# Alternating output banks, two held-back output products and ScalarE's order in block 0, in a fused attention and Strassen MLP kernel

## The chip, the cores and the metric

The kernel runs on one core of one Trainium2 chip. The metric is the device time of one execution in microseconds (us). All times below are in us unless marked otherwise. In times of the trace, zero is the start of the first instruction.

## The reference

The first half is a linear attention without softmax, with a norm per head. Its output is the input of a two-layer MLP with a leaky ReLU.

```python
kv  = einsum('bhsd,bhse->bhde', k, v)          # B=8, H=8, S=576, D=64
o   = einsum('bhsd,bhde->bhse', q, kv)
rms = sqrt(mean(o * o, axis=-1) + 1e-6)
x   = (o / rms * g_norm)                       # -> (B*S, H*D) = (4608, 512)
h   = x @ w_in                                 # w_in (512, 2048)
g   = maximum(0.01 * h, h)
out = g @ w_out                                # w_out (2048, 512)
```

q, k, v and g_norm arrive as float32. The two weight matrices arrive as float64 and the kernel rounds them to float32 itself.

## The kernel before

**Blocks.** The 4608 rows are cut into nine blocks of 512 rows. A *block* goes through the MLP while the attention for the next one is computed in between. All TensorE matmuls are issued through one helper (L118), which pins them: TensorE runs them in exactly the order of the program text. On the other engines a scheduler orders the instructions, apart from those wrapped in `pin(...)`, which keep program order among themselves on their engine.

**Block 0** (`first_block`, L880) is computed directly, in 16 *units* of 128 hidden columns. For unit n TensorE makes `h_ps` (the unit's hidden values, four matmuls of 128x512), ScalarE applies the leaky ReLU (`Prelu`, L898) and writes `g`, and TensorE then adds the unit's part of the output into four accumulators `o_acc`. The program order on TensorE is h_ps of unit n+1, then o_acc of unit n, and so on. So the Prelu of unit n has the time of one o_acc and one h_ps to finish.

**What runs beside block 0.** `between(n, half)` (L922) is called twice per unit. It rounds the weights: each of 32 *roundings* (`round_f64`, L229) takes two ScalarE instructions (`add`, L242, and `cut`, L244) on a raw tile that SP's queue has loaded (L220), and four VectorE instructions (L246, L250, L252, L255). The ScalarE and VectorE instructions of the roundings are pinned. The buffers between the two engines hold four roundings, and the raw tiles hold seven. The loop asks for six roundings after unit 1, three after each of units 2 to 5, then two. `between` also advances the attention of rows 512 to 1151 (`outputs`, L341, and `divide`, L357): TensorE makes `o_ps` (and earlier `kv_ps` from k and v), ScalarE squares it (L349) and scales it (L355), VectorE adds, transposes and reduces the squares (L353, L363, L364), ScalarE takes the root (L367), VectorE the reciprocal (L369), ScalarE spreads it (L373), VectorE transposes and multiplies (L379, L381). L349 and L355 are not pinned. The loads of q, k and v for pairs of heads are on SP's queue too, in program order with the weight loads.

**Blocks 1 to 8** use Strassen's scheme with seven products in place of eight. The 2048 hidden columns are cut into four *chunks*. For each chunk there are seven hidden products (`product_h` for block 1, `product_h_two`, a second level of the scheme, for the others) and seven output products (`product_o`, L836). Both come in the order 1, 2, 6, 5, 7, 3, 4. In the main loop a hidden product and an output product of an earlier chunk alternate, one of each per *slot* (28 slots per block). Output products wait in `o_queue` and are started by `go_o` (L958), with a lag of two slots.

**The banks of the output.** `strassen` (L735) gets two names of PSUM banks. Products 1, 6, 7 and 4 write into the first, products 2, 5 and 3 into the second. Products 1, 2 and 5 start a bank afresh, the others go on in it. After each product VectorE (or, for a chunk's first use in a block, ScalarE, L851) reads the bank and adds it to the output tiles (L582). Before the change the first bank is o_a and the second o_c for every chunk except the very last, which uses hd and hc, two banks of the hidden products. So from chunk to chunk products 4 and 1 use the same bank one after the other.

**The end of a chunk.** When the seven hidden products are done, VectorE combines them, ScalarE applies the leaky ReLU, and GpSimd makes four sums of the result, `gs` (`sums_of`, L760). Products 6, 5, 7 and 3 of the output need these sums; products 1 and 2 don't. In the last block, nothing but output products is left for TensorE after the last hidden product. Loads of the sums of w_out for a later product (`pairs<-w`, L618, on SP's queue) are issued when products 5 and 4 have been read.

Of the kernel before, what the change touches and what calls it, by code (L numbers as in the profile page):

```python
# [12 lines left out]
AF = mybir.ActivationFunctionType  # L13
# [10 lines left out]
def kernel(  # L24
# [36 lines left out]
    nc = tc.nc  # L61
    B, H, S, D = q.shape
# [8 lines left out]
    NB = B * S // NT  # L71
    N2 = NT // 2
    U = 2
    NC = DF // 2 // (U * P)
    SLOPE = 0.01
# [14 lines left out]
    pin = tc.keep_in_program_order  # L90
# [194 lines left out]
    eps_sb = consts.tile([P, 1], F32, name="eps_sb")  # L285
# [40 lines left out]
    def t2k(n, name):  # L326
        home = {"tag": name, "bufs": 1} if name[:3] == "sum" else {"tag": "t2k", "bufs": 3}
        return work.tile([P, n], F32, name=name, **home)

    def x_of(lo, hi):  # L330
        return block(lo // NT)[:, :, lo % NT:lo % NT + hi - lo]
# [25 lines left out]
    def divide(lo, hi, sums):  # L357

        x, n = x_of(lo, hi), hi - lo
        rms = work.tile([P, 2, n // E], F32, tag="rms", name="rms", bufs=2)  # L360
        for l in range(2):
            t = t2k(n, "turned")
            in_turn(nc.vector.transpose(t, sums[l]))  # L363
            in_turn(nc.vector.tensor_reduce(rms[:, l, :], t.rearrange("p (a i) -> p a i", i=E),  # L364
                                            axis=AX.X, op=ALU.add))
            if l:
                nc.scalar.activation(rms, rms, func=AF.Sqrt, scale=1.0 / D, bias=eps_sb)  # L367
            yield
        in_turn(nc.vector.reciprocal(rms, rms))  # L369
        spread = []  # L370
        for l in range(2):
            t = t2k(n, "spread")
            nc.scalar.copy(t.rearrange("p (a i) -> p a i", i=E),  # L373
                           rms[:, l, :].unsqueeze(2).to_broadcast([P, n // E, E]))
            spread.append(t)
        yield
        for l in range(2):
            inv = t2k(n, "inv")
            in_turn(nc.vector.transpose(inv, spread[l]))  # L379
            to = x[:, 2 * l:2 * l + 2, :]  # L380
            in_turn(nc.vector.tensor_mul(to, to, inv.unsqueeze(1).to_broadcast([P, 2, n])))  # L381
            yield
# [453 lines left out]
    def product_o(n, g_sides, os, finish):  # L836
        c = n % NC
        w_sides, _ = sides_w2(n)
        sums = sides_w2(n + 1)[1] if n + 1 < NC * (NB - 1) else lambda i: None
        if c == 0:  # L840
            for key in ("11", "12", "21", "22"):
                os[key] = opool.tile([P, 2, N2], F32, tag="o", name=f"o{key}", bufs=6)

        into = {1: ("11", True), 5: ("22", True), 2: ("11", False), 6: ("12", True),
                3: ("12", False), 7: ("22", False), 4: ("21", True)}

        def done(i, bank):
            key, fresh = into[i]
            to = os[key].rearrange("p u (v n) -> p (u v) n", v=2)
            if c == 0 and fresh:  # L850
                nc.scalar.copy(to, bank)  # L851
            else:
                add(nc.vector, to, bank, to)
            if c == NC - 1 and i in (2, 7, 3, 4):
                finish(key, os[key])

            if i == 5:
                sums(0)
            elif i == 4:
                sums(1)  # L860


        yield from strassen(("oa", "oc") if n + 1 < NC * (NB - 1) else ("hd", "hc"), lambda i, part, r: g_sides[i][:, 2 * r + part, :],
                            lambda i, part, r: w_sides[i][:, r, :], done)

    def go(steps, n=None):
# [13 lines left out]
    def first_block(between):  # L880

        accs = [ps_m.tile([P, DM], F32, tag=t, name="o_acc") for t in ("oa", "oc", "hb", "hd")]
        x, last = xTs.pop(0), None
        for n in range(2 * NC * U + 1):
            now = last
            if n < 2 * NC * U:
                c, h, u = n // (2 * U), n // U % 2, n % U
                h_ps = ps_m.tile([P, NT], F32, tag=("ha", "hc")[n % 2], name="h_ps")

                parts = 2 if n == 0 else 1  # L890
                for part in range(parts):
                    cols = slice(part * NT // parts, (part + 1) * NT // parts)
                    for e in range(NE):
                        matmul(h_ps[:, cols], lhsT=w1_sb[h][c][:, u, e, :],
                               rhs=x[:, e, cols], start=(e == 0 and part == 0),
                               stop=(e == NE - 1), skip_group_check=True)
                gT = view(g_all[n // 4 % 2], n % 4 * NT, NT)
                nc.scalar.activation(gT, h_ps, func=AF.Prelu, alpha=SLOPE)  # L898
                last = (gT, w2_sb[h][c][:, u, :], n)
            if now is None:  # L900
                continue
            between(n, 0)
            for t in range(4):
                matmul(accs[t], lhsT=now[0][:, t * P:(t + 1) * P], rhs=now[1],
                       start=(now[2] == 0), stop=(n == 2 * NC * U))
            between(n, 1)
        for t in range(4):
            o = opool.tile([P, DM], F32, tag="o", name="o", bufs=6)
            if t % 2:
                nc.scalar.copy(o, accs[t])  # L910
            else:
                nc.vector.tensor_copy(o, accs[t])
            nc.scalar.dma_start(out[t * P:(t + 1) * P, :], o)
# [39 lines left out]
    LATE_SLOTS = (3, 4)  # L953

    LAG = 2
    o_queue, waited = collections.deque(), 0

    def go_o():  # L958
# [5 lines left out]
    for i in range(1, NB):  # L964
        one = i == 1
        steady = not one
        late, a_steps = a_steps, attention(i + 1, fine=not one) if i + 1 < B else iter(())
        os = {}
        for c in range(NC):
            g_sides = {}  # L970
            h_steps = product_h(c, h_sides, x_sides, g_sides) if one else \
                product_h_two(i, c, quarters, g_sides)
            for t in range(7):
                slot = 7 * c + t
                go(h_steps, 1)
                if not one:

                    if t == 6:
                        go(h_steps, 1)
                    if slot in LATE_SLOTS:  # L980
                        go(late, 1)
                    for _ in range(FINE_SLOTS.get(slot, 0)):
                        go(a_steps, 1)
                    if i + 1 < NB:
                        if slot == 20:
                            x_sides, new_quarters, sums, inner = sides_x(i + 1)
                        if slot in (20, 21, 22):
                            go(sums, 2 if slot == 20 else 1)
                        if slot == 24:
                            inner(0)  # L990
                        elif slot == 25:
                            inner(1)
                    load_some()
                if waited == LAG:
                    go_o()
                elif o_queue:
                    waited += 1
                if one:

                    if t == 1:  # L1000
                        combine(c, 2)
                    if t == 3 and c < NC - 1:
                        h_sides, more_h = sides_w1(c + 1)
                        combine(c + 1, 0)
                    if t == 5 and c < NC - 1:
                        more_h()
                        combine(c + 1, 1)
                    if slot == 4:
                        go(late, 1)
                    if slot in A_SLOTS:  # L1010
                        go(a_steps, 1)
                    load_some()
                    if slot == 24:
                        go(a_steps)
                        x_sides, new_quarters, sums, inner = sides_x(i + 1)
                        go(sums)
                    elif slot == 25:
                        inner(0)
                    elif slot == 26:
                        inner(1)  # L1020
            if i == NB - 1 and c == NC - 1:
                go(h_steps, 1)
                go_o()
            go(h_steps)
            if c == NC - 1 and i + 1 < NB:
                inner(2)
                quarters = new_quarters
            if one:
                read((2, 4, RING, RING)[c])
            o_queue.append(product_o((i - 1) * NC + c, g_sides, os, store(i)))  # L1030
    while go_o():
        pass
# [30 lines left out]
```

## Time and profile before

| | |
|---|---|
| median of three executions | 942.53 (942.1 to 942.6) |
| the profiled execution: its own time | 942.25 |
| the profiled execution: its span | 940.5 |
| mean granted TensorE clock | 0.998 |
| TensorE busy | 920.1 |
| VectorE busy | 616.0 |
| ScalarE busy | 327.5 |
| GpSimd busy | 317.7 |

The profile comes from one execution, taken by the hardware profiler. A row of the timeline has the start, the time, the engine (PE is TensorE, PEld its weight loads, DVE VectorE, ACT ScalarE, POOL GpSimd, SP the queue of the DMAs), the source line, the operation and what it writes and reads by the program's names, with the idle time before it and who ended that in brackets. A row of the waits has the engine with the tile and line that waited, who it waited for, the total in us, the number of times, and the longest. A row of the windows has the stretch and its length, the busy time and instructions of TensorE, its weight loads, VectorE, ScalarE and GpSimd, then the granted share of the TensorE clock, the share of the DMA engines and the GB/s. The granted clock tells how fast TensorE was allowed to run, 1.00 being full speed.

### The profile page before, as it was taken

What the parts mean: (1) busy time and instruction counts of PE and PEld (TensorE: products, weight loads), DVE (VectorE), ACT (ScalarE), POOL (GpSimd) and SP (SyncE); (2) the same over time, 40 slices, a digit from 0 to 9 for tenths busy, and PEclk for the clock granted to TensorE, in tenths of its full rate; (3) what the DMA queues carried; (4) which work ended last, traced back from release to release, by engine and by line L of the source; (5) the groups of instructions that cost most, each with busy time, mean ns of one, the idle gap of its engine ahead of it and who ended that gap; (6) DMA issues with size and microseconds to landing.
All of it is one profiled execution on the core that took longest, in us unless ns stands there. A gap on an engine that the chain in (4) does not pass through costs nothing.

```text
span 940.5 us, 17989 instructions
## 1 busy us (share of the span) xinstructions
PE 920.1 (98%) x7076; PEld 779.1 (83%) x7076; DVE 616.0 (65%) x992; ACT 327.5 (35%) x659; POOL 317.7 (34%) x318
## 2 busy tenths in 40 slices
PE   7999999999999999999999999999999999999997
PEld 5544447788998899889998999989988999899996
DVE  3866994576457876587657865687558745654554
ACT  3544633242134332533343323342344232223320
POOL 2000364977522532236221611172225322532222
PEclk9999999999999999999999999999999999999999
DMA  8989916885598679856895589658755675567632
GB/s 271 246 211 220 267 61 188 275 296 163 181 312 260 182 211 304 257 164 200 286 287 173 171 280 297 193 169 262 236 154 176 196 219 188 174 199 220 187 108 67
DMA packets 90067, 200.05 MB, mean 213 GB/s; under 512 B 9856, under 2 KB 42112, under 8 KB 89984
## 3 DMA queue, kind: packets, MB, share of 16 engines
q1 hardware_dynamic: 79392, 186.85, 66.3%
q10 hardware_dynamic: 10144, 10.88, 3.4%
q8 instruction: 56, 0.92, 0.4%
q0 software_dynamic: 448, 1.18, 0.3%
q14 instruction: 27, 0.22, 0.1%
HBM read 172.39 MB, written 26.48 MB: 211 GB/s over the span
## 4 chain that ended last, share of the span: by engine, by line
PE 86%; DVE 8%; DMA 3%; issue 1%; POOL 1%; ACT 1%; SPq 0%; DVEq 0%; ACTq 0%; POOLq 0%
PE o_a L118 21%; PE o_c L118 17%; PE h_ha L118 10%; PE h_hc L118 8%; PE h_hb L118 7%; PE h_hd L118 6%; PE o_acc L118 4%; PE h_ps L118 4%; PE kv_ps L118 2%; PE h_c L118 2%; PE h_d L118 2%; PE o_ps L118 1%; PE h_a L118 1%; DMA pairs<-in_v_dram 1%; DVE o L582 1%
## 5 line engine op out<-in xcount | busy, mean ns | idle before, releaser
L582 POOL TENSOR_TENSOR gs<-g 128x512 f32<-128x512 f32 x64 | 81.3, 1289 | 446.7 <-ACT g L753 446.7
L582 DVE TENSOR_TENSOR o<-o_c,o 128x512 f32<-128x512 f32 x85 | 58.5, 688 | 108.2 <-PE o_c L118 108.1
L753 ACT ACTIVATE g<-g 128x512 f32<-128x512 f32 x124 | 78.2, 631 | 122.9 <-DVE g L582 122.9
L118 PE MATMUL o_a<-pairs,gs 128*128 128x256 f32 x496 | 117.3, 379 | 0.0
L582 DVE TENSOR_TENSOR o<-o_a,o 128x512 f32<-128x512 f32 x100 | 68.7, 687 | 71.2 <-PE o_a L118 71.1
L817 ACT COPY w_all<-h_ha 128x512 f32<-128x512 f32 x84 | 48.7, 580 | 189.8 <-PE h_ha L118 181.0
L118 PEld LDWEIGHTS o_a<-pairs,gs 128*128 128x128 f32 x496 | 90.0, 190 | 9.9
L118 PE MATMUL o_a<-w,g 128*128 128x256 f32 x248 | 59.9, 384 | 4.7 <-DVE o L582 4.1
L118 PEld LDWEIGHTS h_ha<-stage,w_all 128*128 128x128 f32 x448 | 58.8, 192 | 2.9
L118 PE MATMUL o_c<-w,g 128*128 128x256 f32 x248 | 59.7, 383 | 0.0
L118 PE MATMUL o_c<-pairs,gs 128*128 128x256 f32 x248 | 59.2, 381 | 0.0
L118 PE MATMUL o_a<-pairs,g 128*128 128x256 f32 x248 | 59.2, 381 | 0.0
L118 PE MATMUL h_ha<-stage,w_all 128*128 128x128 f32 x448 | 59.0, 275 | 0.0
L118 PE MATMUL o_acc<-w,g 128*128 128x512 f32 x128 | 58.3, 598 | 0.7 <-ACT g L898 0.7
L118 PE MATMUL o_c<-w,gs 128*128 128x256 f32 x248 | 58.7, 379 | 0.0
L118 PE MATMUL h_ps<-xT,w_all 128*128 128x512 f32 (+1 forms) x136 | 57.9, 570 | 0.2 <-DVE w_all L255 0.2
L582 DVE TENSOR_TENSOR g<-g,pairs 128x512 f32<-128x512 f32 x84 | 55.6, 689 | 1.9
L118 PEld LDWEIGHTS o_a<-w,g 128*128 128x128 f32 x248 | 44.9, 190 | 13.9 <-DVE o L582 7.8
L582 POOL TENSOR_TENSOR pairs<-w_all 128x512 f32<-128x512 f32 x8 | 11.1, 1383 | 125.7 <-ACT cut L244 106.9
L118 PEld LDWEIGHTS o_c<-w,g 128*128 128x128 f32 x248 | 44.9, 190 | 8.4 <-issue 3.1
L118 PEld LDWEIGHTS o_a<-pairs,g 128*128 128x128 f32 x248 | 45.0, 190 | 6.5 <-DVE w_all L582 0.9
L118 PEld LDWEIGHTS o_c<-pairs,gs 128*128 128x128 f32 x248 | 44.9, 190 | 6.5 <-issue 1.4
(202 smaller groups left out, 1980.6 us busy)
## 6 DMA issues: line engine op xcount, KB each, us to landing
w_all<-w SPq DMA_DIRECT2D x196, 448.0 KB, 4.1
pairs<-w SPq DMA_DIRECT2D x56, 512.0 KB, 4.4
out_dram<-o ACTq DMA_DIRECT2D x36, 256.0 KB, 4.6
v_in<-in_v_dram SPq DMA_DIRECT2D x29, 288.0 KB, 5.3
k_in<-in_k_dram SPq DMA_DIRECT2D x28, 288.0 KB, 5.8
q_in<-in_q_dram SPq DMA_DIRECT2D x56, 144.0 KB, 6.1
q_in<-in_q_dram SPq DMA_DIRECT2D x56, 140.0 KB, 6.0
w<-stage SPq DMA_DIRECT2D x12, 512.0 KB, 4.5
```

The source lines that it names most:

```text
L118: pin(nc.tensor.matmul(*args, **kw))
L582: ins = eng.tensor_tensor(out_, a, b_, op=ALU.subtract if minus else ALU.add)
L753: nc.scalar.activation(t, t if src is None else src, func=AF.Prelu, alpha=SLOPE)
L817: nc.scalar.copy(q[:, at], banks[tag])
```

## The change

It has three parts. The output's two banks swap their roles from chunk to chunk, and the last chunk uses the same two banks as all others. In the last block, slots 22 and 25 start no output product, so the queue is two products longer when the hidden products end. And two kinds of ScalarE instruction are pinned: the Prelu of block 0 (L898) and the root of the norm (L367), which runs in all blocks.

```diff
@@ divide
             if l:
-                nc.scalar.activation(rms, rms, func=AF.Sqrt, scale=1.0 / D, bias=eps_sb)
+                pin(nc.scalar.activation(rms, rms, func=AF.Sqrt, scale=1.0 / D, bias=eps_sb))
@@ product_o
-        yield from strassen(("oa", "oc") if n + 1 < NC * (NB - 1) else ("hd", "hc"), lambda i, part, r: g_sides[i][:, 2 * r + part, :],
+        yield from strassen((("oa", "oc"), ("oc", "oa"))[n % 2], lambda i, part, r: g_sides[i][:, 2 * r + part, :],
                             lambda i, part, r: w_sides[i][:, r, :], done)
@@ first_block
-                nc.scalar.activation(gT, h_ps, func=AF.Prelu, alpha=SLOPE)
+                pin(nc.scalar.activation(gT, h_ps, func=AF.Prelu, alpha=SLOPE))
@@ main loop
+    HELD = (22, 25)
...
-                if waited == LAG:
+                if slot in HELD and i == NB - 1:
+                    pass
+                elif waited == LAG:
                     go_o()
                 elif o_queue:
                     waited += 1
```

## The prediction, made before the result was known

> **What bounds the kernel now.** I read the page first, then the waits of TensorE alone, then the timeline around each of those waits, then the granted clock.
>
> ```profile
> PE 920.1 (98%) x7076; PEld 779.1 (83%) x7076; DVE 616.0 (65%) x992; ACT 327.5 (35%) x659; POOL 317.7 (34%) x318
> ...
> PE o_a L118 <- DVE o L582: 4.1, 6, 1.3
> PE h_d L118 <- POOL gs L582: 2.2, 1, 2.2
> PE o_acc L118 <- ACT g L898: 0.7, 1, 0.7
> PE o_a L118 <- ACT o L851: 0.6, 1, 0.6
> ```
>
> TensorE is the bound. What can be won are its few waits, and whatever makes TensorE wait anew is paid in full: the other engines have no share in the end. Seven of its waits are for bank o_a, one is for the last chunk's sums (gs), one for a Prelu of block 0.
>
> ```profile
> 808.73 0.68 DVE L582 TENSOR_TENSOR o<-o_a,o 128x512 f32<-128x512 f32 x1
> 809.47 1.99 PE L118 MATMUL o_a<-w,g 128*128 128x256 f32 x8 [1.30 <-DVE o L582]
> ...
> 921.76 1.89 PE L118 MATMUL h_c<-w,g 128*128 128x256 f32 x8
> 925.90 3.56 PE L118 MATMUL h_d<-pairs,gs 128*128 128x256 f32 x8 [2.25 <-POOL gs L582]
> 929.30 1.89 PE L118 MATMUL h_c<-pairs,gs 128*128 128x256 f32 x8
> ...
> 922.30:925.60 3.30, 1.35 (x7) 0.84 (x5) 1.04 (x2) 0.00 (x0) 3.30 (x3) 1.00 0.33 131
> 925.70:929.00 3.30, 3.10 (x7) 2.52 (x8) 0.00 (x0) 0.00 (x0) 1.41 (x2) 0.50 0.12 41
> ```
>
> In the two window rows the first number after the length is TensorE's busy time, and the third from the end the granted clock. After the wait of 2.25 the clock is 0.50 for one stretch, and one output product takes 3.40 (925.90 to 929.30) instead of 1.72 (929.30 to the next at 931.02). The waits near 1.4 left the clock at 1.00.
>
> Block 0, where the third part of the change works:
>
> ```profile
> 49.39 0.34 PE L118 MATMUL o_ps<-qT,kv 64*32 64x64 f32 x16
> 49.66 3.70 PE L118 MATMUL o_acc<-w,g 128*128 128x512 f32 x8
> 56.72 0.34 PE L118 MATMUL o_ps<-qT,kv 64*32 64x64 f32 x16
> ...
> 42.63 0.60 ACT L898 ACTIVATE g<-h_ps 128x512 f32<-128x512 f32 x1 [2.84 <-PE h_ps L118]
> ...
> 49.99 0.33 ACT L349 ACTIVATE sum<-o_ps 128x64 f32<-128x64 f32 x2
> 50.20 0.68 ACT L242 ACTIVATE add<-stage 128x512 uint32<-128x512 uint32 x1
> 50.75 0.67 ACT L244 ACTIVATE cut<-stage 128x512 f32<-128x512 f32 x1
> 51.32 0.51 ACT L355 ACTIVATE xT<-o_ps,g_sb 128x64 f32<-128x64 f32 x2
> ...
> 141.53 0.30 ACT L367 ACTIVATE rms<-rms,eps_sb 128x8 f32<-128x8 f32 x1 [8.05 <-DVE rms L364]
> 142.10 0.50 ACT L373 COPY spread<-rms 128x128 f32<-128x128 f32 x2 [0.27 <-DVE rms L369]
> 142.51 0.59 ACT L898 ACTIVATE g<-h_ps 128x512 f32<-128x512 f32 x1
> ```
>
> Here h_ps and o_acc follow each other on TensorE, 3.43 each, almost without a gap. The Prelu of unit n (g<-h_ps, L898) must be done when o_acc of unit n starts, one o_acc and one h_ps later (6.9 of slack). ScalarE works strictly down its queue: at 141.53 a root waited 8.05 for VectorE, and the Prelu behind it came at 142.51, late.
>
> **The banks.** Product 4 of a chunk and product 1 of the next both used o_a. Alternating, product 1 finds a bank that was read one product earlier. The seven waits go: 4.1 + 0.6 = 4.7, and the refill after each (1.99 for a product started after a wait, 1.89 else: 7 x 0.10 = 0.7), 5.4 in all. Next in line is product 2 on the bank that product 4 left: 3.4 later, and the late read of 808.73 ends at 809.41, before 811.5, where product 2 would start. So I count the whole 5.4; its other bound is 0, if VectorE's lateness only moves to another bank.
>
> **The held products.** At the end five output products run after the last hidden product (ends 915.01) until the first that needs the sums of the last chunk; the sums are done 10.83 after it (925.84). With two held back there are seven, 7 x 1.72 = 12.04, and the hidden products and the sums come 3.44 earlier. The wait and the slow clock go: 2.25 + (3.40 - 1.72) = 3.93. New on that path: the last product now shares o_a and o_c with the one before, where it had banks of its own. VectorE reads product 7 after three additions of 0.69: at 6.98 after the last hidden product, while product 4 wants that bank at 6.89: 0.15 lost with the signal. Gain 3.8. Bounds: 2.0 (a wait of the same kind as at 808.73, 1.4, at one more place) and 3.9. The loads of the sums of w2 on SP's queue (L618, 4.4 to landing) move with the products that issue them: the tightest is issued at 920.4, lands at 924.8 and is first used at 927.2. Hidden.
>
> **ScalarE's order in block 0.** The edit pins L898 and L367 among instructions already pinned (the roundings, L242 and L244). In the built queue, the Prelu of unit 2 now stands behind all six roundings that the loop issues before it, while the squares and scalings of the attention (L349, L355), not pinned, stay where the scheduler put them: *ahead* of roundings 9 and 10, thus ahead of the Prelu of unit 2. But they read o_ps, which TensorE makes after h_ps of unit 3, just ahead of the o_acc that waits for this Prelu. So ScalarE stands idle until o_ps ends, then does two squares (0.21 apart), a scaling (0.20), a rounding (two instructions, 1.13), a scaling (0.20), a rounding (1.13) and the Prelu (0.60): 3.47. With 0.12 from TensorE's end to ScalarE (as at 108.07 + 0.98 to 109.17), 0.05 back, and 0.34 - 0.27 of o_ps itself: 3.7 of idle TensorE.
> Unit 3 has the same fault: squares, two scalings, one rounding, Prelu: 0.21 + 0.40 + 1.13 + 0.60 + 0.24 = 2.6.
> Units 4 to 7 I walked down both queues (2.25 of VectorE per rounding, four roundings of buffers in flight; 2.3 per weight load to land, 5.2 per pair of heads): their Prelus come 2.9, 4.7, 1.2 and 5.3 ahead of need. Unit 8's stands behind roundings 25 and 26, whose loads follow two pairs of heads on SP's queue; these start only when kv_ps has freed their tiles. 0.7 (75.64 to the issue at 76.36) + 2.0 of latency (an estimate: 256 KB alone landed in 2.2) + 10.3 for the pairs (81.59 to 91.85) + 2.6 + 2.1 for the two loads (to 94.47 and 96.57) puts the last landing 17.7 after kv_ps, rounding and Prelu at 19.5; o_acc of unit 8 is due at 18.4 (five half-units of 3.43 and the next kv_ps, 1.2). Wait 1.05. Bounds: 0, if the queue is empty sooner, and 4.3, if they land as late as before (kv_ps ended 75.64, second load landed 96.57: 20.9). Later units are on time.
> The root that held unit 15's Prelu now stands behind it: its wait goes, 0.9 with the refill (0.7 as bound). In five later blocks the root moves behind two copies (0.59, 0.48); the reciprocals that need it came 1.1 to 3.1 after it: hidden.
>
> **The clock.** A wait of 3.7 and one of 2.6 are longer than the tail's 2.25. Each can leave up to one slow stretch of 3.4, a loss of 1.7; where the edges of the stretches fall decides. I take 1.4 for the first and 0.9 for the second (of the 2.6, one stretch must hold nearly 2: so for about half of the positions), 2.3 together; bounds 0 and 3.4.
> The Trainium skill, "TensorE: Matmul & The Clock Gate", section "HAM oscillation — how this bites in real kernels", warns of gaps over about 3.4 us. Here 2.25 were enough, so the row decides; by the page the first wait alone would cost, the clock term were about 1.4 and the sum about 0.9 lower.
>
> **The sum.** Block 0: 3.7 + 2.6 + 1.05 + 2.3 - 0.9 = +8.75. Banks -5.4, tail -3.8. Net -0.45. The profiled execution took 942.25 (span 940.5 and 1.75 around it), 0.28 below the median 942.53; from the median, 942.1. That is no change: 0.2% is 1.9 us, about what a measurement of this kernel can tell.
>
> **Rivals.**
> *A, slower: the third late Prelu is a long one.* The loads behind the pairs of heads land 20.9 after kv_ps as before. Wait 4.3 instead of 1.05, with a slow stretch of its own, 1.7: net +4.5, 947.0. It decides from about 18.5 on. For it: the row of before. Against: three loads that were still under way then (until 81.59, 6 after kv_ps) have now landed earlier.
> *B, faster: TensorE's new waits cost no clock and unit 8 is on time.* Then 8.75 becomes 5.4: net -3.8, 938.7. For it: waits of 1.4 cost none. Against: the tail.
> *C, faster by all its gains: the Prelus are not late.* Net -10.1, 932.4. It would take o_ps not to stand in front of the Prelu; the built order says it does.
> *D, slower: the alternation wins nothing,* because VectorE's late reads hold the next product on the other bank: net +4.95, 947.5. Against: 811.5 above.
>
> **How the numbers follow.** No change 0.43; A 0.22, D 0.08; B 0.22, C 0.05. Faster 0.27, same 0.43, slower 0.30. The likeliest case alone holds 940.6 to 944.4. For 8 in 10 the range reaches to A and B, 938.6 to 947.0; C and what lies past A are left out.
>
> **What would show it.** In the profile after: no wait of an output product for VectorE at a chunk's start; no slow clock after 900; seven o products in a row there. In block 0, o_acc waiting for L898 twice, 3.7 and 2.6, each time just after o_ps, and half clock after the first at least; perhaps a third wait near 100 to 106. No wait before the last o_acc. I am wrong if the Prelus of units 2 and 3 run before the squares, or if a further unit (6 has the least margin, 1.2) is late too.

## The result, and the profile after

The changed kernel took 941.11 us (median of four executions, 939.05 to 941.45). The kernel before took 942.57 beside it (four, 942.1 to 943.77). The medians differ by 1.5 us. The ratio on record, 0.9978 with a 95% interval of 0.9961 to 0.9995, is not their quotient (0.9985); by it the change wins 2.1 us. Both are about the 0.2% that the text above calls the edge of what can be told. The profiled execution took 940.91, its span is 939.2; before, these were 942.25 and 940.5.

So a change with three working parts moved the time by almost nothing. First the waits of TensorE, the view that carried the prediction:

```profile
PE o_acc L118 <- ACT g L898: 6.1, 2, 3.6
...
PE h_b L118 <- ACT g L778: 0.4, 1, 0.4
```

The waits for o_a are gone, and so is the one for gs. In their place o_acc waits twice for the Prelu (L898), 6.1 in all. One small wait is new that the prediction does not name: h_b for a copy of ScalarE (L778), in block 1.

The timeline of ScalarE and of TensorE around the first of the two waits, in the changed kernel:

```profile
51.26 0.34 ACT L349 ACTIVATE sum<-o_ps 128x64 f32<-128x64 f32 x2 [8.90 <-PE o_ps L118]
51.49 0.32 ACT L355 ACTIVATE xT<-o_ps,g_sb 128x64 f32<-128x64 f32 x1
51.68 0.67 ACT L242 ACTIVATE add<-stage 128x512 uint32<-128x512 uint32 x1
52.23 0.67 ACT L244 ACTIVATE cut<-stage 128x512 f32<-128x512 f32 x1
52.78 0.33 ACT L355 ACTIVATE xT<-o_ps,g_sb 128x64 f32<-128x64 f32 x1
52.98 0.69 ACT L242 ACTIVATE add<-pairs 128x512 uint32<-128x512 uint32 x1
53.53 0.69 ACT L244 ACTIVATE cut<-pairs 128x512 f32<-128x512 f32 x1
54.08 0.62 ACT L898 ACTIVATE g<-h_ps 128x512 f32<-128x512 f32 x1
```

```profile
50.83 0.34 PE L118 MATMUL o_ps<-qT,kv 64*32 64x64 f32 x16
54.76 5.33 PE L118 MATMUL o_acc<-w,g 128*128 128x512 f32 x8 [3.58 <-ACT g L898]
59.93 3.60 PE L118 MATMUL h_ps<-xT,w_all 128*128 128x512 f32 x8
63.45 0.34 PE L118 MATMUL o_ps<-qT,kv 64*32 64x64 f32 x16
66.29 3.70 PE L118 MATMUL o_acc<-w,g 128*128 128x512 f32 x8 [2.49 <-ACT g L898]
```

ScalarE stands idle for 8.90 until o_ps is there, then works off squares, scalings and roundings, and the Prelu comes last. TensorE has nothing to do meanwhile: its next instruction, o_acc, needs that Prelu. The o_acc after the first wait takes 5.33 in place of 3.70; the granted clock beside it is 0.50 (the windows stand in the last section). The one after the second wait takes 3.70.

The end of the changed kernel, on TensorE:

```profile
913.11 0.83 PE L118 MATMUL h_hb<-stage,w_all 128*128 128x128 f32 x6
913.78 1.89 PE L118 MATMUL o_a<-pairs,gs 128*128 128x256 f32 x8
...
918.96 1.89 PE L118 MATMUL o_c<-w,gs 128*128 128x256 f32 x8
920.98 1.99 PE L118 MATMUL o_a<-pairs,g 128*128 128x256 f32 x8
...
926.27 1.89 PE L118 MATMUL o_c<-pairs,gs 128*128 128x256 f32 x8
```

After the last hidden product, seven output products run from 913.78 until 926.27, where the first product that needs the last sums starts (12.5 for seven: 1.73 each, the one gap below and the refill of 0.1 behind it), and nothing waits for gs. The only gap is at 920.98, where the product starts 2.02 after the one before instead of 1.73: 0.29 for product 4's bank, which VectorE was still reading (its read of o_a runs from 920.24 to 920.92).

Where the 1.3 us of span came from was found by setting the starts of the same TensorE instructions of both executions against each other, one by one. In us, minus is earlier than before:

| where | predicted | measured |
|---|---|---|
| seven bank waits | -5.4 | -5.5 |
| tail | -3.8 | -3.8 |
| Prelu of unit 2 | +3.7 | +3.7 |
| Prelu of unit 3 | +2.6 | +2.6 |
| Prelu of unit 8 | +1.05 | 0 |
| wait of the last o_acc (unit 15) | -0.9 | -0.9 |
| half clock in block 0 | +2.3 | +1.6 |
| h_b in block 1 | not named | +0.5 |
| kv_ps at 174, waiting for a load of v | not named | -0.9 |
| start-up, before the first h_ps | not named | +1.4 |
| sum | -0.45 | -1.3 |

The start-up is not work of the change: it runs before any of its instructions, and it came 0.6 to 2.9 later than before in the kernels below too, whatever they changed. It goes with the clock that was granted there: the execution of before has no stretch at half clock in its start-up, that of the changed kernel has one (17.12 to 20.54). Below, the kernel with none is 0.8 late, those with one 0.6 to 1.6, those with two 1.8 to 2.9. The wait of kv_ps for the load was anything from nothing to 0.97 in them; the paragraph on h_b comes back to it.

Unit 8, to which the prediction gave a third wait, has none. Its Prelu ends at 101.01, and its o_acc starts 2.4 later:

```profile
100.44 0.57 ACT L898 ACTIVATE g<-h_ps 128x512 f32<-128x512 f32 x1
...
103.43 3.70 PE L118 MATMUL o_acc<-w,g 128*128 128x512 f32 x8
```

### The profile page after: what moved, and what is told of

The parts are those of the page before. It is cut to its first block, busy times and chain, and to the rows that moved or that the text cites. A ratio compares the mean times of both kernels' runs of the same rounds, so it can differ in the third digit from the quotient of the medians.

```text
span 939.2 us, 18015 instructions
## 1 busy us (share of the span) xinstructions
PE 921.9 (98%) x7076; PEld 780.0 (83%) x7076; DVE 612.9 (65%) x992; ACT 328.2 (35%) x659; POOL 317.5 (34%) x318
## 3 DMA queue, kind: packets, MB, share of 16 engines
q0 software_dynamic: 448, 1.18, 0.3%
## 4 chain that ended last, share of the span: by engine, by line
PE 91%; DVE 1%; ACT 0%; issue 0%; DVEq 0%
PE o_a L118 21%; PE o_c L118 21%; PE h_ha L118 11%; PE h_hb L118 8%; PE h_hc L118 8%; PE h_hd L118 6%; PE o_acc L118 5%; PE h_ps L118 4%; PE o_ps L118 2%; PE kv_ps L118 2%; PE h_a L118 1%; PE h_b L118 1%; PE h_c L118 1%; PE h_d L118 1%; DVE g L582 0%; DVE xT L381 0%
## 5 line engine op out<-in xcount | busy, mean ns | idle before, releaser
L582 DVE TENSOR_TENSOR o<-o_c,o 128x512 f32<-128x512 f32 x104 | 71.6, 689 | 111.1 <-PE o_c L118 111.1
L753 ACT ACTIVATE g<-g 128x512 f32<-128x512 f32 x124 | 78.2, 631 | 121.4 <-DVE g L582 121.4
L582 DVE TENSOR_TENSOR o<-o_a,o 128x512 f32<-128x512 f32 x88 | 60.5, 687 | 68.3 <-PE o_a L118 68.1
L118 PE MATMUL o_c<-pairs,gs 128*128 128x256 f32 x384 | 91.3, 381 | 0.0
L118 PE MATMUL o_a<-pairs,gs 128*128 128x256 f32 x384 | 90.8, 379 | 0.0
L118 PEld LDWEIGHTS o_c<-pairs,gs 128*128 128x128 f32 x384 | 69.8, 190 | 9.3 <-issue 1.4
L118 PEld LDWEIGHTS o_a<-pairs,gs 128*128 128x128 f32 x384 | 69.8, 190 | 7.8
L118 PE MATMUL o_c<-w,g 128*128 128x256 f32 x256 | 61.6, 383 | 0.0
L582 POOL TENSOR_TENSOR pairs<-w_all 128x512 f32<-128x512 f32 x8 | 10.5, 1313 | 140.5 <-DMA pairs<-in_moe_w_in_dram 92.8
L118 PEld LDWEIGHTS o_acc<-w,g 128*128 128x128 f32 x128 | 24.5, 195 | 36.3 <-issue 29.6
L118 PEld LDWEIGHTS h_ps<-xT,w_all 128*128 128x128 f32 x136 | 25.5, 190 | 29.2 <-issue 26.5
L582 DVE TENSOR_TENSOR w_all<-h_hc,w_all 128x512 f32<-128x512 f32 x56 | 38.4, 686 | 15.5 <-PE h_hc L118 15.3
```

The source lines that it names most:

```text
L118: pin(nc.tensor.matmul(*args, **kw))
L582: ins = eng.tensor_tensor(out_, a, b_, op=ALU.subtract if minus else ALU.add)
L753: nc.scalar.activation(t, t if src is None else src, func=AF.Prelu, alpha=SLOPE)
```

## The experiments

The theory: two parts win about 9 us, and the pins of block 0 lose about as much, because squares and scalings that are *not* pinned stand ahead of the pinned Prelu on ScalarE and need an o_ps that TensorE makes just before it stops. Rivals: the parts don't add (one gives only what another takes); the pinned Prelu is late because of the roundings in front of it, whose loads and buffers pace it; or it is the pinned root that costs.

Eight kernels ran, in two sets of four. The sets ran on different chips, each with its own runs of the kernel before (942.31 in the first set, 943.35 in the second, 17 executions each), so ratios are compared across them and not times.

### One part at a time

The first kernel is the changed one without the two pins, banks and held products kept:

```diff
-                pin(nc.scalar.activation(rms, rms, func=AF.Sqrt, scale=1.0 / D, bias=eps_sb))
+                nc.scalar.activation(rms, rms, func=AF.Sqrt, scale=1.0 / D, bias=eps_sb)
...
-                pin(nc.scalar.activation(gT, h_ps, func=AF.Prelu, alpha=SLOPE))
+                nc.scalar.activation(gT, h_ps, func=AF.Prelu, alpha=SLOPE)
```

> The alternating banks and the held products, without the two pins. In the built order, ScalarE's queue in block 0 is then that of the kernel before. Theory (the parts add, and the pins are what eats the gain): 5.4 from the banks and 3.8 from the end, so about 933.3 against 942.5 before; no o_acc waits for the Prelu of units 2 and 3, the one wait of 0.7 at the last o_acc stays. Rival (the pins cost little, the banks or the end win less than thought): 940 to 942, as with all three parts.

The second is the changed one with the banks as before and `HELD` empty, so with the pins alone:

```diff
-        yield from strassen((("oa", "oc"), ("oc", "oa"))[n % 2], ...
+        yield from strassen(("oa", "oc") if n + 1 < NC * (NB - 1) else ("hd", "hc"), ...
...
-    HELD = (22, 25)
+    HELD = ()
```

> The two pins alone; banks and end as before. Theory: units 2 and 3 wait 3.7 and 2.5 with at least one stretch of half clock (1.7), the wait at the last o_acc is gone (0.9), block 1 is about even: 942.5 + 7.0 = 949.5, or 947.8 to 951.2 with no or two slow stretches. The waits for o_a and for gs stay. Rival (the late Prelus show in the trace but other work makes up for them): 942 to 944.

The third is the kernel before with the new line of `strassen`, so the banks alone:

```diff
-        yield from strassen(("oa", "oc") if n + 1 < NC * (NB - 1) else ("hd", "hc"), ...
+        yield from strassen((("oa", "oc"), ("oc", "oa"))[n % 2], ...
```

> The alternating banks alone. Theory: the seven waits for o_a go and none comes in their place: 942.5 - 5.4 = 937.1; the wait of 2.2 for gs and the slow clock at the end stay. Rival (VectorE is late as before, so the next product on the other bank waits): 941 to 942.5, with waits of o_a or o_c elsewhere in the chunk.

The fourth is the kernel before with the new test in the main loop, so the held products alone (the last chunk keeps hd and hc):

```diff
-                if waited == LAG:
+                if slot in HELD and i == NB - 1:
+                    pass
+                elif waited == LAG:
```

> The two held products alone, with the last chunk on hd and hc as before. Theory: the wait for gs and the slow clock at the end go, 942.5 - 3.9 = 938.6; the seven waits for o_a stay. Rival (the end needs the alternating banks as well, since the held products queue up on o_a and o_c): 940.5 or more, with a new wait of o_a or o_c for VectorE after 905.

Measured, with the ratio to the kernel before and its 95% interval:

| kernel | median us (range, executions) | ratio | span |
|---|---|---|---|
| banks and held, no pins | 934.53 (933.4 to 935.78, 6) | 0.9914 [0.9898, 0.9929] | 931.7 |
| pins only | 948.26 (947.58 to 950.58, 6) | 1.0063 [1.0047, 1.0079] | 946.4 |
| banks only | 936.53 (935.46 to 940.67, 6) | 0.9939 [0.992, 0.9959] | 935.3 |
| held only | 939.60 (938.34 to 942.58, 12) | 0.9975 [0.9962, 0.9988] | 937.2 |

The parts add: -0.61 - 0.25 + 0.63 = -0.23%, and all three together gave -0.22%. Banks with held products gave -0.86%, the sum of the two. (Each interval is 0.13 to 0.2% to either side, so a part of 0.2% or so that only appears in company would not show in these sums.) So the small result is two gains and a loss that happen to cancel, and not three edits without effect.

Setting the TensorE starts against those of before gives -5.5 for the banks in the banks-only kernel (2.0 late at kv_ps, 3.5 early at the last o_a) and the two kernels without them keep the six waits of o_a for VectorE, 4.1 in all, as before. One expectation for the banks-only kernel failed in its profiled execution: at the end it waits 1.8 for gs and 0.2 for a Prelu, yet no half clock follows (TensorE was busy for 2.01 of the stretch with the wait). The pins-only kernel shows the two waits of block 0, to the hundredth:

```profile
52.28 0.34 PE L118 MATMUL o_ps<-qT,kv 64*32 64x64 f32 x16
56.21 3.70 PE L118 MATMUL o_acc<-w,g 128*128 128x512 f32 x8 [3.58 <-ACT g L898]
...
63.27 0.34 PE L118 MATMUL o_ps<-qT,kv 64*32 64x64 f32 x16
66.11 2.41 PE L118 MATMUL o_acc<-w,g 128*128 128x512 f32 x5 [2.49 <-ACT g L898]
```

They are 3.58 and 2.49, as in the changed kernel. (The last row is cut off by the end of the view, with five of eight matmuls.) Yet here the o_acc after the first takes 3.70, not 5.33: the same wait was followed by half clock there and not here. The last section comes back to that.

### Which of the instructions on ScalarE makes the Prelu late

The changed kernel with squares and scalings pinned as well (in all blocks, since they share these two lines):

```diff
-            nc.scalar.activation(sq, o_ps[l], func=AF.Square)
+            pin(nc.scalar.activation(sq, o_ps[l], func=AF.Square))
...
-            nc.scalar.activation(x[:, 2 * l + e, :], o_ps[l], func=AF.Copy, scale=g_sb[:, e:e + 1])
+            pin(nc.scalar.activation(x[:, 2 * l + e, :], o_ps[l], func=AF.Copy, scale=g_sb[:, e:e + 1]))
```

> The changed kernel, with the squares (L349) and the scalings (L355) of block 0 kept in program order as well, so that on ScalarE they stand behind the Prelus of units 2 and 3 and not ahead of them; the Prelus keep their place behind the roundings. My theory (a Prelu is late because squares that need o_ps stand ahead of it): the waits of 3.6 and 2.5 us vanish, no half clock in block 0, about 934 (932.5 to 936). Rival (the pinned Prelu is late because it stands behind the roundings, whose loads and buffers pace it): the two waits stay, about 941.

Banks, held products, and the Prelu pinned, the root free:

```diff
-                pin(nc.scalar.activation(rms, rms, func=AF.Sqrt, scale=1.0 / D, bias=eps_sb))
+                nc.scalar.activation(rms, rms, func=AF.Sqrt, scale=1.0 / D, bias=eps_sb)
```

> Banks and held products, and of the pins only that of the Prelu (L898); the root (L367) is free again. My theory: the waits of 3.6 and 2.5 stay; the Prelu of unit 15 stands behind the root again or not, by the place that the scheduler gives the root; the wait of h_b for the copy L778 in block 1 (0.6) is gone, since it was the moved root that shifted the queue there. About 941 (939.5 to 942.5). Rival (the pinned root makes the Prelus late): no waits of 3.6 and 2.5, about 934.

Banks, held products, and the root pinned, the Prelu free:

```diff
-                pin(nc.scalar.activation(gT, h_ps, func=AF.Prelu, alpha=SLOPE))
+                nc.scalar.activation(gT, h_ps, func=AF.Prelu, alpha=SLOPE)
```

> Banks and held products, and of the pins only that of the root (L367). My theory: no waits of 3.6 and 2.5 in block 0, the wait of the last o_acc in block 0 (0.9) gone, that of h_b in block 1 (0.6) there: about 934.2 (932.5 to 936), 0.3 under banks and held products without any pin. Rival (the root is what costs): about 941.

As the last, but the root pinned only for the rows of the first sequence:

```diff
-                pin(nc.scalar.activation(rms, rms, func=AF.Sqrt, scale=1.0 / D, bias=eps_sb))
+                root = nc.scalar.activation(rms, rms, func=AF.Sqrt, scale=1.0 / D, bias=eps_sb)
+                if lo < S:
+                    pin(root)
```

> As the kernel with only the root pinned, but pinned in block 0 alone and left to the scheduler in the blocks behind. My theory: the wait of the last o_acc in block 0 (0.9) is gone, and the wait of h_b in block 1 (0.6) as well: about 933.6 (932 to 935.5), the shortest of these four by a little. Rival (the wait in block 1 follows from the pin in block 0, which moves the whole queue behind it): the wait of h_b stays, 934.2.

| kernel (all with banks and held products) | median us (range, executions) | ratio | span |
|---|---|---|---|
| Prelu, root, squares and scalings pinned | 935.03 (933.69 to 939.24, 6) | 0.9915 [0.9894, 0.9937] | 932.0 |
| Prelu pinned | 944.08 (942.27 to 946.27, 12) | 1.0007 [0.9995, 1.002] | 942.6 |
| root pinned | 933.46 (932.07 to 934.89, 5) | 0.989 [0.9873, 0.9908] | 930.7 |
| root pinned for the first sequence | 934.24 (933.79 to 935.5, 4) | 0.9899 [0.9883, 0.9915] | 932.8 |

**The cause is the squares and scalings ahead of the Prelu, shown by adding pins.** With everything pinned, the Prelu still stands behind the roundings, but the squares stand behind the Prelu:

```profile
46.67 0.59 ACT L898 ACTIVATE g<-h_ps 128x512 f32<-128x512 f32 x1
...
52.86 0.67 ACT L244 ACTIVATE cut<-pairs 128x512 f32<-128x512 f32 x1
53.44 0.58 ACT L898 ACTIVATE g<-h_ps 128x512 f32<-128x512 f32 x1
53.91 0.33 ACT L349 ACTIVATE sum<-o_ps 128x64 f32<-128x64 f32 x2
54.12 0.53 ACT L355 ACTIVATE xT<-o_ps,g_sb 128x64 f32<-128x64 f32 x2
```

The two rows of L898 are the Prelus of units 2 and 3. The first ends at 47.26, and its o_acc starts at 51.94 without a wait; both waits of block 0 are gone, and with them 0.6% of the time (0.9978 to 0.9915). The rival that blames the roundings needed about 941. Squares and scalings were pinned together; which of the two would do alone is not shown.

**The root alone is harmless, the Prelu alone is worse than the two together.** With only the Prelu pinned the second wait is longer than in the changed kernel (3.87, not 2.49). ScalarE before it:

```profile
64.35 0.34 ACT L349 ACTIVATE sq<-o_ps 128x64 f32<-128x64 f32 x2 [7.01 <-PE o_ps L118]
64.57 0.52 ACT L355 ACTIVATE xT<-o_ps,g_sb 128x64 f32<-128x64 f32 x2
65.53 0.30 ACT L367 ACTIVATE rms<-rms,eps_sb 128x4 f32<-128x4 f32 x1 [0.44 <-DVE rms L364]
66.07 0.39 ACT L373 COPY spread<-rms 128x64 f32<-128x64 f32 x2 [0.24 <-DVE rms L369]
66.37 0.65 ACT L242 ACTIVATE add<-pairs 128x512 uint32<-128x512 uint32 x1
66.93 0.65 ACT L244 ACTIVATE cut<-pairs 128x512 f32<-128x512 f32 x1
67.48 0.58 ACT L898 ACTIVATE g<-h_ps 128x512 f32<-128x512 f32 x1
```

The free root and the spreading now stand ahead of the Prelu too, and the chain through VectorE between them is waited for: 1.4 more. In the changed kernel the pin on the root had kept these out. My expectation here, 941, missed by 3 us: 1.4 of the wait, and in the profiled execution half clock after both waits, not one. (The kernel before took 943.35 in this set, 0.8 more than beside the changed kernel.) The last o_acc doesn't wait here, though the root is free: TensorE comes there later than before, and ScalarE, past the root, stands idle for 2.50 until the h_ps of unit 15 is done.

**Where the wait of h_b comes from.** It is there in every kernel with the root pinned throughout (also with pins only) and in no other. The copy L778 reads the bank of h_b, and the next product on that bank has to wait for it. The place on ScalarE in block 1, with the root pinned:

```profile
158.09 0.28 ACT L367 ACTIVATE rms<-rms,eps_sb 128x8 f32<-128x8 f32 x1
...
162.80 0.63 ACT L753 ACTIVATE g<-g 128x512 f32<-128x512 f32 x1 [2.00 <-DVE g L582]
163.34 0.57 ACT L778 COPY g<-h_b 128x512 f32<-128x512 f32 x1
```

and without any pin:

```profile
161.61 0.60 ACT L753 ACTIVATE g<-h_a 128x512 f32<-128x512 f32 x1 [0.37 <-PE h_a L118]
163.34 0.59 ACT L778 COPY g<-h_b 128x512 f32<-128x512 f32 x1 [1.13 <-PE h_b L118]
```

The pin moves one root (128x8) from block 0, where it held up the Prelu of unit 15, into block 1. VectorE's work on that root (the reciprocal, transposes and products of L369, L379 and L381) moves with it. With the root pinned it runs from 158.40 to 162.16, ahead of the addition g<-h_c, which starts at 162.09, 3.6 after h_c is done; without pins the addition starts at 159.89, 0.04 after h_c. A Prelu of block 1 (L753) waits 2.00 for this addition, the copy L778 stands behind that Prelu, and TensorE waits for the copy. In its place this costs 0.5, and the move wins 0.9. Whether all of the 0.5 reaches the end is not shown: 11 us later kv_ps waits 0.2 to 1.0 for a load in the kernels without the wait of h_b, and not at all in three of the four kernels with it (0.5 with the pins only).

**The last of the four did not do what it was made for.** The 128x8 root belongs to the second sequence (rows 576 to 1151), so its pin was gone and the order there was as with no pins: the wait of the last o_acc stayed (0.9), that of h_b went. It says nothing about a pin on that one root alone.

The shortest is the kernel with banks, held products and the root pinned, 0.989 of before. Its interval overlaps those of no pins, all pins and the last one; a gain of 0.4 over no pins follows from the two waits in the traces (0.9 less, 0.5 more), and the times alone don't show it. All four are faster than the changed kernel by 0.6% to 0.9%.

## Why the prediction was right, step by step

The time (942.1 against 941.11) and the case "no change" came out, and the two large gains and the two large losses behind them as well. That the sum came so close is in part luck: unit 8 and the clock were set 1.75 too high together, and three terms that the prediction doesn't name (start-up, h_b, kv_ps) came to +1.0. The steps:

- **Banks, counted whole at 5.4:** right, 5.5. The read of product 4 that was late at 808.73 before is just as late in the changed kernel, where it starts at 812.67, now on o_c. Product 1 has started on o_a at 811.95 without a wait. The read ends at 813.35, and product 2, the next on o_c, starts at 815.24, as was argued with 811.5 on the clock of before.
- **Tail, 3.8:** right against the profiled execution (3.8), with the new wait mis-sized (0.15 predicted, 0.29 measured). But as a gain of the kernel it was set too high: the held products alone gave 0.25%, 2.4 us (1.1 to 3.6). The term 3.40 - 1.72 for half clock was taken as certain because the profile of before showed it. In the pins-only kernel a wait of 2.24 at the same place was followed by full clock, so it is a loss that comes in some executions.
- **Prelus of units 2 and 3, 3.7 and 2.6:** right, 3.7 and 2.6. Reading the built queue against TensorE's order gave the place, and durations of the rows gave the size.
- **Margins of units 4 to 7 (2.9, 4.7, 1.2, 5.3):** measured 3.1, 4.6, 1.6 and 5.7, from the end of each Prelu to the start of its o_acc.
- **Unit 8, 1.05:** wrong; it was 2.4 early. The last rounding's load landed 14.3 after kv_ps, not 17.7. The terms at fault are the durations of loads, taken from a row of before in which three other loads were still under way. In the changed kernel SP's queue had nothing in flight when it started the pairs of heads. They were issued 0.1 after kv_ps (0.7 in the sum), the last landed 10.5 later (95.52; 2.0 + 10.3 in the sum), and the two weight loads took 3.7 more (2.6 + 2.1). Rounding and Prelu (1.8) and the time at which o_acc is due (18.6 against 18.4) were right. The text named the empty queue as an argument against rival A and used it for the start of the loads, but not for how long they take.
- **Unit 15, -0.9:** right. But the root that stood ahead of it was followed only as far as "hidden" in later blocks. It moved work in block 1, and the 0.5 of h_b is the price there. The reciprocals that need the root were looked at; the additions of VectorE that then stand behind them were not. The pin isn't the only thing that ends the wait: with the Prelu alone pinned it was gone too, as told above.
- **Clock, 2.3:** the first wait lost 1.6 where 1.4 was taken, the second nothing where 0.9 was taken. The bounds 0 and 3.4 both turn up in profiled executions: 0 with the pins only, half clock after both waits with only the Prelu pinned.
- **The rule weighed against the row:** the Trainium skill, "TensorE: Matmul & The Clock Gate", section "HAM oscillation — how this bites in real kernels", warns of gaps over about 3.4 us. That gave the first wait alone, and so it came in this one trace. The other traces decide against it as a rule: 3.58 was followed by full clock in one, 2.25 by half clock in another.

Rival C, at 932.4, had the right mechanism for another kernel: once the Prelus were not late, the time was 0.989 to 0.9915 of before (932.2 to 934.5 from 942.53). Rivals A and D did not occur. B is half true: unit 8 was on time, but the first wait did cost clock.

## What to carry to other kernels

A pin orders an instruction among the *pinned* ones only; what is left free keeps the place that the scheduler gave it, and can end up ahead of the pinned instruction with a need that comes later. Before an activation on the bound engine's path is pinned, list what the built queue has ahead of it and when each of those can start; here either all neighbours had to be pinned, or the Prelu left free. And when several edits go in together, run them apart: two of these were worth 0.86%, and the third gave most of it back.

## What the runs showed of the hardware

**The clock is granted by a fixed raster, not by the length of a wait.** In all traces the granted clock changes at multiples of 3.41 us from each other: in the changed kernel at 17.12, 20.54, 54.67 and 58.08, which is 1, 10 and 1 times 3.41 apart, and before at 925.69 and 929.11. Cut at these edges, the stretches around the waits read as follows (columns as in the prediction). Before, at the tail:

```profile
922.28:925.69 3.41, 1.37 (x7) 0.86 (x5) 1.06 (x2) 0.00 (x0) 3.41 (x3) 1.00 0.35 137
925.70:929.11 3.41, 3.21 (x8) 2.59 (x9) 0.00 (x0) 0.00 (x0) 1.41 (x2) 0.50 0.12 39
```

The changed kernel, both waits of block 0:

```profile
51.25:54.66 3.41, 0.00 (x0) 0.00 (x0) 1.62 (x4) 3.40 (x10) 0.00 (x0) 1.00 0.82 154
54.67:58.08 3.41, 3.32 (x4) 1.51 (x5) 3.27 (x7) 2.27 (x5) 0.00 (x0) 0.50 0.68 162
61.49:64.90 3.41, 2.31 (x21) 0.75 (x19) 1.27 (x7) 1.00 (x5) 0.00 (x0) 1.00 1.04 288
64.91:68.32 3.41, 2.03 (x5) 1.06 (x6) 2.59 (x7) 3.41 (x7) 0.00 (x0) 1.00 1.06 238
```

The pins alone, the first wait of block 0 and the tail:

```profile
50.85:54.26 3.41, 1.77 (x20) 0.56 (x18) 0.00 (x0) 1.55 (x6) 0.00 (x0) 1.00 1.01 215
54.27:57.68 3.41, 1.47 (x4) 0.76 (x5) 3.12 (x7) 3.41 (x8) 0.00 (x0) 1.00 0.64 180
57.69:61.09 3.40, 3.40 (x10) 1.49 (x9) 3.26 (x6) 0.72 (x2) 0.00 (x0) 1.00 0.99 231
931.49:934.90 3.41, 1.56 (x7) 1.40 (x8) 0.34 (x1) 0.00 (x0) 3.07 (x3) 1.00 0.22 77
934.91:938.31 3.40, 3.40 (x17) 2.99 (x17) 1.38 (x2) 0.00 (x0) 0.00 (x0) 1.00 0.00 0
```

Of these stretches at full clock, those in which TensorE was busy for 1.37 or less are followed by one at half clock, those with 1.47 or more are not. The wait of 3.58 fell into one stretch in the changed kernel and was cut in two (1.64 and 1.94 idle) with the pins alone, so it cost 1.6 in the first and nothing in the second. With the Prelu pinned alone the stretches before the two half-clock ones were busy for 0.49 and 1.18 us:

```profile
52.22:55.63 3.41, 0.49 (x1) 0.30 (x2) 2.21 (x5) 3.41 (x8) 0.00 (x0) 1.00 1.04 224
...
65.88:69.29 3.41, 1.18 (x3) 0.68 (x4) 2.72 (x9) 3.22 (x8) 0.00 (x0) 1.00 0.89 193
```

So in these executions the limit lies between 40% and 43% of a stretch for these matmuls. In the start-up, with other shapes, a stretch busy for 45% was followed by half clock (1.52, only the Prelu pinned), and two with 46% and 49% were not (1.58 and 1.68, only the root pinned). The raster does not start with the kernel: its edges lay differently in each execution.

The Trainium skill, "TensorE: Matmul & The Clock Gate", section "What's actually happening", says that the window of 3413 ns runs freely, and these traces agree; it puts the fall to half clock after an idle window, and here a window 60% idle was enough.

Much of the scatter of the kernel before goes with this. One stretch at half clock lowers the mean clock over 939 us by 0.0018 and costs 1.7. The 17 executions of the kernel before in the first set had a mean clock of 0.998 (eight of them, 940.4 to 942.3), 0.997 (one, 942.6), 0.996 (four, 942.3 to 943.0) or 0.994 (four, 944.1 to 944.6). It isn't all of the scatter: with everything pinned, two executions with the same mean clock of 0.996 took 933.69 and 939.24, and the cause of that is open. What one profiled execution shows of the clock is thus one draw. As an estimate, the gain of a wait that is removed is the wait, plus 1.7 times the share of positions in which one stretch holds about 2 us of it.
